# New keys for single tasks of a planned kernel, packed chunks of x, and a state update in column halves

## The chip, the cores and the metric

The kernel runs on one NeuronCore of a Trainium2 chip. Five engines work from queues of their own: TensorE (PE in the profile; PEld is its weight load), VectorE (DVE), ScalarE (ACT), GpSimd (POOL) and SyncE (SP), which here issues every DMA. The metric is the device time of one execution in microseconds (us), as a median of runs.

## The reference

The program is a gated linear recurrence over 768 steps for 4 batches of 8 heads (head size 48), and behind it a feed-forward layer without a token mixer:

```python
for t in range(S):
    state = alpha[:, :, t, :, None] * state + np.einsum('bhd,bhe->bhde', k[:, :, t], v[:, :, t])
    y[:, :, t] = np.einsum('bhd,bhde->bhe', q[:, :, t], state)
x = y.transpose(0, 2, 1, 3).reshape(B * S, H * D)      # 3072 x 384
h = x @ w_in                                           # 384 -> 2048
g = h * np.tanh(log1p(exp(h)))
out = g @ w_out                                        # 2048 -> 384
```

The weights arrive as 64-bit floats.

## The kernel before

**Chunks.** Time is cut into chunks of 128 steps, six for each of the four batches; the 24 chunks go by number n, batches innermost, so chunks 0 to 3 begin the four batches. For a chunk, q, k and alpha of all heads arrive as one tile `qka` (112 partitions, 1541 numbers each) and v as another. VectorE makes the running products of alpha with two scans: `rest` (L492) from the chunk's end and the front one (L509); it multiplies k (L504, two halves) and q (L519) by them. TensorE makes scores (L539, 16 small matmuls), VectorE masks them (L549, two instructions), TensorE makes the product y (L594; 16 matmuls in the first chunk of a batch, 24 later). For the next chunk the state is advanced: TensorE turns k (L702), ScalarE copies it out (L706), TensorE multiplies it with v (L711, four matmuls whose 112x96 results hold two heads each, of which only the two blocks on the diagonal are wanted), and two instructions (L721 on ScalarE in a batch's first chunk, L723 on VectorE later) gather the diagonal blocks into the state.

**x in two parts.** y is kept as an upper part (rounded, L611) and a lower part (what is left). In chunks 0 to 7 the lower part is made by TensorE (L623) and ScalarE (L631), later by VectorE (L616). The rows of the last head pair are then moved to other partitions by six DMAs a chunk (L637), 16 KB each. Only then can the chunk's matmuls with w_in begin.

**Weights.** For each of 16 tiles f of 128 hidden columns, a DMA (L349) brings both weight matrices' parts; VectorE makes 32-bit floats from the 64-bit words in three steps (L364, L369, L374), ScalarE rounds an upper part (L379), and the lower part comes from TensorE and ScalarE (L403, L404, L407) for f < 4, from VectorE (L393) for the others. The weights are loaded a second time later (L422), and ScalarE checks them (L431, L434).

**Units.** A unit is two or four chunks of x by one tile f: nine matmuls with w_in into a PSUM bank `h` (L754; there are two such banks), five ScalarE and three VectorE instructions for the activation (L762 to L788; L762 and L772 are the ones that read the bank), and three matmuls with w_out for each chunk (L816) that add into the banks `o0` to `o3`. There are 106 units: 20 of two chunks, then 86 of four.

**Order.** No loop sets the order. All of this is first recorded as tasks, each with an engine, a cost, a time after which its result is there, and a key. `Plan.order` then plays a clock: on each engine it looks at the first 150 waiting tasks by key and takes the one that can begin first (the earlier key where two can), writes down the order, and the kernel issues the instructions in it. The engines then run it strictly in that order. Where TensorE would be idle between `FILL_FROM` and `FILL_UNTIL` the planner puts a matmul on zeros in (a fill, L866), which computes nothing. `EARLY_BANKS` gives the PSUM banks of the first chunks by hand. A DMA is a task of SP with a fixed cost and a fixed delay.

Of the kernel before, what the change touches and what calls it, by code (L numbers as in the profile page):

```python
# [37 lines left out]
QKA = (3 * C + 1) * NPAIR + 1  # L38

# [26 lines left out]
EARLY_BANKS = {
    0: "o2 h o3 o0 att att".split(),
    1: "att att att att o3 att".split(),
    2: "o0 h h h att o1".split(),
    3: "o3 h att o1 att o0".split(),  # L70
    4: "att att att att o1 h".split(),
    5: "o2 o3 att o2 o2 att".split(),
}
# [7 lines left out]
BEGIN = {"PE": 2.4, "DVE": 4.3, "ACT": 2.2, "POOL": 4.2, "SP": 1.2}  # L81
# [17 lines left out]
class Plan:  # L99
# [23 lines left out]
    def order(self):  # L123
# [95 lines left out]
WINDOW = 150  # L219

COST = {
    "load part": (0.7, 3.3), "load q": (1.8, 5.0), "load v": (0.7, 4.0), "load w": (2.0, 5.0),
    "move": (0.63, 2.5), "store": (0.47, 3.0),
    "cold fill": (0.321, 0.36), "fill": (0.1635, 0.2), "off": (0.2, 0.35), "w off": (0.95, 1.2), "lead": (0.27, 0.38), "bits": (0.47, 0.58), "w hi": (0.42, 0.56), "w lo": (0.95, 1.08),
# [3 lines left out]
    "scores": (1.07, 1.08), "y0": (1.08, 1.1), "y": (1.7, 1.7), "turn": (0.4, 0.64),  # L228
    "turned": (0.43, 0.57), "update": (0.76, 0.98),
# [14 lines left out]
def fast_path(ctx, tc, qka, v, w, out, good):  # L244
# [57 lines left out]
    xs = [const.tile([P, 2, NPAIR, k * C], F32R, name=f"xs{i}") for i, k in enumerate(X_TILES)]  # L302
# [40 lines left out]
    def weight(f):  # L343
        key = weight_unit[f] - W_LEAD
# [9 lines left out]
        got = add("SP", *COST["load w"], max(key, FIRST_W + f) - 4, load, uses=[stage])  # L354
        fs = slice(f * P, (f + 1) * P)
        for m in range(2):
# [29 lines left out]
            k = key + 0.5 * m  # L386
# [29 lines left out]
    def weight_check(f):  # L416
        key = CHECK_FROM + f * CHECK_STEP
# [30 lines left out]
    def attention(n):  # L448
# [3 lines left out]
        st, key = state[b], due[n]  # L452
# [23 lines left out]
        if n == 0:  # L476
# [7 lines left out]
        got_v = add("SP", *COST["load v"], key - V_LEAD, load_v, uses=[v_buf])  # L484
# [255 lines left out]
    def unit(c0, nt, f, at, ends):  # L740
        N, key = nt * C, float(at)
# [398 lines left out]
```

## Time and profile before

| | |
|---|---|
| median of three runs | 524.3 us (522.8 to 524.36) |
| the profiled execution's own time | 526.62 us |
| its span, first to last instruction | 524.9 us |
| PE busy | 513.0 us, 98% of the span |
| DVE busy | 382.3 us, 73% |
| ACT busy | 397.3 us, 76% |
| matmuls on zeros (L866) | 43 |

Busy time of PE counts every matmul from its issue to its modelled end, the ones on zeros too, and matmuls overlap; so the share of 98% says that PE has nearly always something in it, not that it could not be faster. What counts is how far apart the starts are. Durations below come from the profiled execution.

### The profile page before, as it was taken

Reading aid. Unit: us, or ns where it says so; the run is one execution under the profiler, and the core shown is the slowest. Engines: PE = TensorE matmul, PEld = TensorE weight load, DVE = VectorE, ACT = ScalarE, POOL = GpSimd, SP = SyncE. Lnnn points to the kernel's source line nnn. Section 1 sums busy time; section 2 is a strip of 40 time slices with the busy share of each in tenths; the row PEclk is TensorE's granted clock in tenths of the full one; section 3 lists DMA queues with packets and bytes.
Section 4 is the critical chain, followed back from the end, with each engine's and each line's share of the span. In section 5 each row is a group of like instructions: output and inputs, shape, how many; then the busy total and the mean of one; then the engine's idle time right before and its main releaser. Section 6 shows DMA issues by size and latency. Waiting matters only on the chain.

```text
span 524.9 us, 11178 instructions
## 1 busy us (share of the span) xinstructions
PE 513.0 (98%) x4287; PEld 447.7 (85%) x4287; DVE 382.3 (73%) x743; ACT 397.3 (76%) x914; POOL 4.6 (1%) x34
## 2 busy tenths in 40 slices
PE   6999999999999999899999999999999999999996
PEld 4678989998898888788899888899988899999996
DVE  6899999999976876868777566886468654554452
ACT  1578789999699987888867856577776567787774
POOL 2000000000000000000000000000000000000000
PEclk9799999999999999999999999999999999999999
DMA  8656636413254866465320132220042000010001
GB/s 269 179 172 195 200 82 205 166 61 116 68 177 139 233 229 191 169 204 162 112 76 0 47 92 76 76 76 1 1 136 78 9 9 2 15 46 1 1 1 65
DMA packets 21818, 54.31 MB, mean 103 GB/s; under 512 B 4000, under 2 KB 14752, under 8 KB 21760
## 3 DMA queue, kind: packets, MB, share of 16 engines
q1 hardware_dynamic: 21760, 53.55, 33.2%
q8 instruction: 35, 0.57, 0.5%
q14 instruction: 23, 0.19, 0.1%
HBM read 46.45 MB, written 4.72 MB: 97 GB/s over the span
## 4 chain that ended last, share of the span: by engine, by line
PE 79%; DMA 8%; DVE 7%; SPq 3%; issue 2%; ACT 2%; DVEq 0%; ACTq 0%
PE bank L816 33%; PE bank L754 32%; DMA qka<-in_qka_dram 8%; PE bank L594 5%; PE bank L539 3%; SPq L637 2%; PE bank L711 2%; PE bank L702 1%; PE bank L403 1%; DVE rest L492 1%; DVE qka L509 1%; DVE t L781 1%; DVE y L772 1%; DVE g L788 1%; DVE xs L616 1%
## 5 line engine op out<-in xcount | busy, mean ns | idle before, releaser
L816 PE MATMUL bank<-wo,g 128*128 128x384 f32 x1152 | 227.4, 341 | 0.2 <-DVE part L843 0.2
L754 PE MATMUL bank<-xs,wi 128*128 128x512 f32 (+1 forms) x954 | 217.8, 373 | 1.8 <-DVE y L772 1.8
L816 PEld LDWEIGHTS bank<-wo,g 128*128 128x128 f32 x1152 | 198.3, 188 | 7.6 <-DVE part L843 0.4
L754 PEld LDWEIGHTS bank<-xs,wi 128*128 128x128 f32 x954 | 167.4, 188 | 28.9 <-DVE y L772 2.1
L762 ACT ACTIVATE u<-bank 128x512 f32<-128x512 f32 (+1 forms) x106 | 58.9, 555 | 82.7 <-PE bank L754 82.4
L772 DVE SCALAR_TENSOR_TENSOR y<-u,bank 128x512 f32<-128x512 f32 (+1 forms) x106 | 66.8, 631 | 49.2 <-ACT u L762 48.8
L788 DVE TENSOR_TENSOR g<-t,g 128x512 fp32r<-128x512 f32 (+1 forms) x106 | 67.2, 635 | 48.0 <-ACT g L785 47.8
L775 ACT ACTIVATE t<-t,tenth 128x512 f32<-128x512 f32 (+1 forms) x106 | 72.0, 679 | 2.3
L781 DVE SCALAR_TENSOR_TENSOR t<-y,t 128x512 f32<-128x512 f32 (+1 forms) x106 | 67.0, 633 | 5.1 <-ACT t L778 4.3
L768 ACT ACTIVATE t<-u 128x512 f32<-128x512 f32 (+1 forms) x106 | 62.6, 590 | 3.7 <-DVE g L788 1.4
L785 ACT ACTIVATE g<-t 128x512 fp32r<-128x512 f32 (+1 forms) x106 | 61.5, 581 | 5.1 <-DVE t L781 3.2
L778 ACT ACTIVATE t<-t 128x512 f32<-128x512 f32 (+1 forms) x106 | 61.6, 581 | 0.5
L492 DVE TENSOR_TENSOR_SCAN rest<-qka,behind 112x516 f32<-112x516 f32 x24 | 29.5, 1228 | 15.2 <-DMA qka<-in_qka_dram 15.2
L509 DVE TENSOR_TENSOR_SCAN qka<-qka,ahead 112x516 f32<-112x516 f32 x24 | 29.4, 1223 | 0.0
L549 DVE COPY_PREDICATED probs<-causal,bank 128x384 f32<-128x384 uint32 x48 | 25.8, 584 | 4.4 <-PE bank L539 4.1
L594 PEld LDWEIGHTS bank<-probs,v 128*64 128x64 f32 (+3 forms) x768 | 20.6, 128 | 8.5 <-issue 3.9
L594 PE MATMUL bank<-probs,v 128*64 128x64 f32 (+3 forms) x768 | 25.5, 227 | 1.5 <-DVE ahead L497 1.5
L539 PEld LDWEIGHTS bank<-qka 48*64 48x64 f32 x768 | 18.6, 137 | 5.8 <-issue 3.7
L539 PE MATMUL bank<-qka 48*64 48x64 f32 (+1 forms) x768 | 22.3, 255 | 0.0
L762 ACT ACTIVATION_READ_ACCUMULATOR u<-bank 128x1 f32 x106 | 20.7, 195 | 0.0
L611 ACT ACTIVATE xs<-bank 112x256 fp32r<-112x256 f32 x48 | 16.3, 373 | 5.6 <-PE bank L594 5.6
L711 PEld LDWEIGHTS bank<-v,ks 128*112 128x112 f32 x160 | 18.0, 177 | 1.8 <-ACT xs L631 0.5
(79 smaller groups left out, 348.4 us busy)
## 6 DMA issues: line engine op xcount, KB each, us to landing
qka<-in_qka_dram SPq DMA_DIRECT2D x23, 674.2 KB, 5.5
ws<-in_wp_dram SPq DMA_DIRECT2D x16, 768.0 KB, 4.6
wc<-in_wp_dram SPq DMA_DIRECT2D x16, 768.0 KB, 5.1
v<-in_vp_dram SPq DMA_DIRECT2D x24, 192.0 KB, 4.6
out_dram<-osb SPq DMA_DIRECT2D x16, 192.0 KB, 1.8
xs<-xs SPq DMA_DIRECT2D x144, 16.0 KB, 2.5
out_dram<-part SPq DMA_DIRECT2D x8, 192.0 KB, 3.1
qka<-in_qka_dram SPq DMA_DIRECT2D x2, 224.0 KB, 3.7
```

The source lines that it names most:

```text
L539: nc.tensor.matmul(p[a][to, i, blocks], K()[r : r + D, j, to], q.rearrange("p (x t) -> p x t", t=HALF), start=True, stop=True,)
L594: made = nc.tensor.matmul(o, l, r, start=begins, stop=m >= len(ops) - 2, skip_group_check=True)
L754: nc.tensor.matmul(p[:, :N], wi[:, z, s, fs], x[:, a, s], start=m == 0, stop=m == len(passes) - 1)
L762: nc.scalar.activation(wide(u), wide(h), AF.Exp, scale=-1.0, accum_out=uchk[:, at : at + 1])
L768: nc.scalar.activation(wide(t), wide(u), AF.Square, bias=1.0, scale=2.0)
L772: nc.vector.scalar_tensor_tensor(wide(y), wide(u), 0.5, wide(h), ALU.add, ALU.mult)
L775: nc.scalar.activation(wide(t), wide(t), AF.Ln, bias=tenth, scale=0.1)
L778: nc.scalar.activation(wide(t), wide(t), AF.Exp, scale=-1.0)
L781: nc.vector.scalar_tensor_tensor(wide(t), wide(y), 0.4, wide(t), ALU.mult, ALU.mult)
L785: nc.scalar.activation(g.tile[:, 0, :N], wide(t), AF.Copy)
L788: late[mybir.EngineType.DVE] = nc.vector.tensor_tensor(g.tile[:, 1, :N], wide(t), g.tile[:, 0, :N].bitcast(F32), ALU.subtract)
L816: made = nc.tensor.matmul(o.tile[:, :DM], g.tile[:, a, j * C : (j + 1) * C], wo[:, z, f], start=begins and m == 0, stop=end and m == 2,)
```

## The change

- **Keys.** A table `SHIFT` adds a number to the keys of single chunks, units, weight tiles and second weight loads. `EARLY_BANKS` has other banks and two more chunks.
- **DMAs in the planner.** A load's delay is no longer fixed: the planner adds up the transfers in their order and lets no more than eight be under way. Costs are changed to match.
- **Loads.** Chunk 1's `qka` is loaded in two parts, alpha first. The rows of `qka` in DRAM lie 1664 numbers apart and no longer 1541.
- **x.** A chunk's upper and lower part now lie next to each other in `xs`, so a move (L637 before, L667 now) takes one run of 256 numbers a partition instead of two of 128. The matmuls with w_in read x in pieces of 128 columns that are 256 apart.
- **State update.** Each pair's matmul with a 112x96 result is cut into two with results of 64x48 and 48x48, each from half the columns of k. The wanted blocks then stand in the same columns, and one gather of 112x192 takes the place of two of 48x192.
- **Weights.** The lower parts come from TensorE for f < 3 instead of f < 4; for f = 3 VectorE makes them.

The order of instructions as built, with chunk numbers as in the words; `qka_116` is chunk 0's tile, `qka_128` (before) and `qka_120` (after) are chunk 1's, `v_124` is chunk 0's v, `v_139` and `v_130` chunk 1's, `ws` are weight loads. SP from its first DMA on, before:

```order
L470 DMA qka_116<-in_qka_dram 112x517
L470 DMA qka_116<-in_qka_dram 112x512 x2
L474 DMA v_124<-in_vp_dram 128x384
L465 DMA qka_128<-in_qka_dram 112x1541
L474 DMA v_139<-in_vp_dram 128x384
L349 DMA ws_145<-in_wp_dram 128x1536
L349 DMA ws_179<-in_wp_dram 128x1536
L465 DMA qka_218<-in_qka_dram 112x1541
```

The same place after:

```order
L498 DMA qka_116<-in_qka_dram 112x517
L498 DMA qka_116<-in_qka_dram 112x512 x2
L498 DMA qka_120<-in_qka_dram 112x517
L502 DMA v_124<-in_vp_dram 128x384
L498 DMA qka_120<-in_qka_dram 112x1024
L502 DMA v_130<-in_vp_dram 128x384
L377 DMA ws_135<-in_wp_dram 128x1536
L377 DMA ws_139<-in_wp_dram 128x1536
L493 DMA qka_217<-in_qka_dram 112x1541
```

Chunk 1's alpha moved ahead of chunk 0's v; the rest keeps its order.

PE around its first unit, before: `qka_313` is chunk 3's tile, `w_lead_1_363` weight tile 1's and `w_lead_0_439` weight tile 2's.

```order
L403 MATMUL bank<-w_lead_1_363,ident 128x384
L404 MATMUL bank<-wo,minus_ident 128x384
L539 MATMUL bank<-qka_313 64x128 x2
L539 MATMUL bank<-qka_313 64x64 x2
L539 MATMUL bank<-qka_313 64x2x64 x2
L539 MATMUL bank<-qka_313 64x64 x2
L539 MATMUL bank<-qka_313 64x128 x2
L539 MATMUL bank<-qka_313 64x64 x2
L539 MATMUL bank<-qka_313 64x2x64 x2
L539 MATMUL bank<-qka_313 64x64 x2
L754 MATMUL bank<-xs_111,wi 128x256 x9
L403 MATMUL bank<-w_lead_0_439,ident 128x384
```

The same place after, from the end of chunk 2's state update on: `v_226` and `ks_351` are chunk 2's, `w_lead_1_371` weight tile 1's, `qka_323` chunk 3's.

```order
L743 MATMUL bank<-v_226,ks_351 64x48
L743 MATMUL bank<-v_226,ks_351 48x48
L782 MATMUL bank<-xs_111,wi 128x256 x9
L653 MATMUL bank<-xs_111,minus_ident 112x256 x2
L431 MATMUL bank<-w_lead_1_371,ident 128x384
L432 MATMUL bank<-wo,minus_ident 128x384
L570 MATMUL bank<-qka_323 64x128 x2
L570 MATMUL bank<-qka_323 64x64 x2
L570 MATMUL bank<-qka_323 64x2x64 x2
L570 MATMUL bank<-qka_323 64x64 x2
```

The first unit moved from behind chunk 3's scores to ahead of chunk 2's lower part, of weight tile 1 and of those scores. Over the whole program 36 matmuls on zeros stand in PE's order after, 43 before.

SP where chunk 13's `qka` is loaded, before (`qka_2772`; `wc` are second weight loads):

```order
L422 DMA wc_2665<-in_wp_dram 128x1536
L422 DMA wc_2702<-in_wp_dram 128x1536
L637 DMA xs_111<-xs_111 16x2x128 x6
L465 DMA qka_2772<-in_qka_dram 112x1541
L474 DMA v_2806<-in_vp_dram 128x384
```

The same place after (`qka_2735`):

```order
L450 DMA wc_2634<-in_wp_dram 128x1536
L450 DMA wc_2688<-in_wp_dram 128x1536
L667 DMA xs_111<-xs_111 16x256 x6
L493 DMA qka_2735<-in_qka_dram 112x1541
L450 DMA wc_2749<-in_wp_dram 128x1536
```

Six moves still stand ahead of the load; a second weight load moved in behind it, ahead of v. The diff, cut to its core:

```diff
+QKA_ROW = 1664
...
-COLD = 16
+COLD = 14
...
-    0: "o2 h o3 o0 att att".split(),
+    0: "att o0 o2 att o3 att".split(),
...
+SHIFT = {
+    "chunk": {
+        4: -3, 5: -1, 6: 1, 7: 3, 8: -0.1, 12: 0.01, 20: 2.5, 21: 1,
...
-W_PE = 4
-W_DVE = 4
+W_PE = 3
+W_DVE = 3
...
+                    if e == "SP" and len(landed) >= QUEUE:
+                        r = max(r, landed[-QUEUE])
...
+            if e == "SP":
+                moving = max(moving, at + DMA_FIRST) + t.late
+                landed.append(moving + DMA_LAST)
+                t.late = moving + DMA_LAST - at
...
-    xs = [const.tile([P, 2, NPAIR, k * C], F32R, name=f"xs{i}") for i, k in enumerate(X_TILES)]
+    xs = [const.tile([P, NPAIR, k, 2, C], F32R, name=f"xs{i}") for i, k in enumerate(X_TILES)]
...
-        st, key = state[b], due[n]
+        st, key = state[b], due[n] + SHIFT["chunk"].get(n, 0.0)
...
-            nc.sync.dma_start(t, qka[b, c])
+            nc.sync.dma_start(t, qka[b, c, :, :QKA])
...
+        elif n == 1:
+            got_a = add("SP", *COST["load part"], -98.7, load_part(2 * NPAIR * C, QKA), uses=[q_buf])
+            got_k = got_q = add("SP", *COST["load qk"], -98.5, load_part(0, 2 * NPAIR * C), uses=[q_buf])
...
-                    x[48 + r : 64 + r, :, s, tok].bitcast(F32),
-                    x[r + 16 * s : r + 16 * s + 16, :, NK, tok].bitcast(F32),
+                    x[48 + r : 64 + r, s, place].bitcast(F32),
+                    x[r + 16 * s : r + 16 * s + 16, NK, place].bitcast(F32),
...
-                nc.tensor.matmul(
-                    p[:R, j, : 2 * D], ks_buf.tile[:, j], V()[:, 2 * D * j : 2 * D * (j + 1)],
-                    start=True, stop=True,
-                )
...
+                for a, wide in ((0, HALF), (1, D)):
+                    h = (2 * j + a) * D
+                    nc.tensor.matmul(
+                        p[64 * a : 64 * a + wide, j, :D], ks_buf.tile[:, j, 64 * a : 64 * a + wide],
+                        V()[:, h : h + D], start=True, stop=True,
+                    )
+
+        def gather():
+            u = by_pair(u_buf.tile)[:R, :, :D]
+            if first:
+                nc.scalar.copy(by_head, u)
+            else:
+                nc.vector.tensor_tensor(by_head, u, by_head, ALU.add)
...
-                    p[:, :N], wi[:, z, s, fs], x[:, a, s], start=m == 0, stop=m == len(passes) - 1
+                    p[:, :N], wi[:, z, s, fs], x[:, s, :, a], start=m == 0,
+                    stop=m == len(passes) - 1,
...
-    qka = np.zeros((B, NCH, R, QKA), inputs["q"].dtype)
+    qka = np.zeros((B, NCH, R, QKA_ROW), inputs["q"].dtype)
```

## Rows read from the trace of the kernel before

**Rows 1.** The page, busy time of the engines
```profile
PE 513.0 (98%) x4287; PEld 447.7 (85%) x4287; DVE 382.3 (73%) x743; ACT 397.3 (76%) x914; POOL 4.6 (1%) x34
```

**Rows 2.** Windows: length, busy time by engine, granted clock, DMA share, GB/s
```profile
12.10:20.60 8.50, 8.40 (x82) 5.35 (x82) 7.03 (x15) 3.75 (x10) 0.00 (x0) 0.60 0.53 146
...
31.30:180.00 148.70, 148.70 (x1348) 133.81 (x1347) 139.67 (x302) 131.56 (x337) 0.53 (x6) 1.00 0.49 154
```

**Rows 3.** Timeline of PE to 48 us: start, length, engine, line, count, [idle]
```profile
12.15 1.06 PE L594 MATMUL bank<-probs,v 128*64 128x64 f32 x32 [1.53 <-DVE ahead L497]
...
15.61 1.56 PE L539 MATMUL bank<-qka 48*64 48x128 f32 x32
...
32.67 1.34 PE L754 MATMUL bank<-xs,wi 128*128 128x256 f32 x9
...
43.55 0.81 PE L403 MATMUL bank<-w_lead,ident 128*128 128x384 f32 x2
...
44.46 0.66 PE L594 MATMUL bank<-qka,state 48*48 48x128 f32 x16
...
46.04 0.91 PE L403 MATMUL bank<-w_lead,ident 128*128 128x384 f32 x2
...
46.97 0.40 PE L623 MATMUL bank<-xs,minus_ident 112*112 112x256 f32 x2
```

**Rows 4.** Timeline of DVE to 40 us, three of its waits from chunk 1 on
```profile
9.93 1.23 DVE L492 TENSOR_TENSOR_SCAN rest<-qka,behind 112x516 f32<-112x516 f32 x1 [2.23 <-DMA qka<-in_qka_dram]
...
17.24 1.05 DVE L549 COPY_PREDICATED probs<-causal,bank 128x384 f32<-128x384 uint32 x2 [0.76 <-PE bank L539]
...
25.95 1.06 DVE L549 COPY_PREDICATED probs<-causal,bank 128x384 f32<-128x384 uint32 x2 [0.87 <-PE bank L539]
```

**Rows 5.** DMA issues from 0.8 to 0.9, and from 2.6 to 3.0 us: size, us to landing
```profile
qka<-in_qka_dram SPq DMA_DIRECT2D x1, 226.2 KB, 2.9
...
qka<-in_qka_dram SPq DMA_DIRECT2D x1, 674.2 KB, 7.2
```

**Rows 6.** Who waited for whom, PE: total us, times, longest
```profile
PE bank L754 <- DVE y L772: 1.8, 1, 1.8
...
PE bank L702 <- DVE xs L616: 0.9, 3, 0.4
```

**Rows 7.** Timelines of SP, DVE and PE around 200 to 213 us
```profile
199.73 5.07 SPq L637 DMA_DIRECT2D xs<-xs  x6
204.91 0.52 SPq L465 DMA_DIRECT2D qka<-in_qka_dram  x1
...
210.61 1.23 DVE L492 TENSOR_TENSOR_SCAN rest<-qka,behind 112x516 f32<-112x516 f32 x1 [3.65 <-DMA qka<-in_qka_dram]
...
202.76 2.25 PE L816 MATMUL bank<-wo,g 128*128 128x384 f32 x12
204.94 0.90 PE L539 MATMUL bank<-qka 48*64 48x128 f32 x32
205.77 4.40 PE L754 MATMUL bank<-xs,wi 128*128 128x512 f32 x18
```

**Rows 8.** Timeline of PE, a state update (L711) and its neighbours at 220 us
```profile
220.62 2.25 PE L816 MATMUL bank<-wo,g 128*128 128x384 f32 x12
222.70 2.24 PE L754 MATMUL bank<-xs,wi 128*128 128x512 f32 x9
...
226.75 0.93 PE L711 MATMUL bank<-v,ks 128*112 128x96 f32 x8
227.46 0.77 PE L816 MATMUL bank<-wo,g 128*128 128x384 f32 x3
```

**Rows 9.** The gathers by line and form: count, busy us, mean ns, idle
```profile
L723 DVE TENSOR_TENSOR state<-bank,state 48x192 f32<-48x192 f32 x32 | 11.3, 352 | 5.9 <-PE bank L711 5.7
```

**Rows 10.** Timelines: DVE's last lower part of w_in, PE's first use of it
```profile
149.39 0.56 DVE L393 TENSOR_TENSOR wi<-w_lead,wi 128x384 fp32r<-128x384 f32 x1
...
153.63 1.55 PE L754 MATMUL bank<-xs,wi 128*128 128x512 f32 x6
```

More of the change, by code (lines that the diff above doesn't have):

```diff
@@ L61 @@
 CHECK_STEP = 2.0
-COLD = 16
+COLD = 14
 FILL_BANKS = ("o3", "o2", "o1", "o0", "h", "att")
-FILL_FROM, FILL_UNTIL = 2.4, 130.0
+FILL_FROM, FILL_UNTIL = 2.5, 130.0
 FILL_MARGIN = 0.1
 EARLY_BANKS = {
-    0: "o2 h o3 o0 att att".split(),
[L68 to L72, printed above, removed]
+    0: "att o0 o2 att o3 att".split(),
+    1: "att att o3 o0 att att".split(),
+    2: "o2 att o0 att h att".split(),
+    3: "att o3 att h h o1".split(),
+    4: "att o3 att att att att".split(),
+    5: "att att att o3 att att".split(),
+    6: "att att att att h o1".split(),
+    7: "att att att att o0 o2".split(),
+}
+SHIFT = {
+    "chunk": {
+        4: -3, 5: -1, 6: 1, 7: 3, 8: -0.1, 12: 0.01, 20: 2.5, 21: 1,
+    },
+    "unit": {
[3 rows of a table added]
+    },
+    "weight": {
+        0: -3, 1: -1, 2: 1.5, 3: 1.1, 4: 5.7, 7: 2, 9: 5, 10: -2, 11: 2, 12: 0.3, 13: 0.5, 15: 2,
+    },
+    "weight check": {
+        5: 9.5, 6: 10, 7: -12, 8: -2, 9: 6, 10: -5,
+    },
 }
 X_PE = 8
-W_PE = 4
-W_DVE = 4
+W_PE = 3
+W_DVE = 3
 W_PE_BANKS = ["o2"]
@@ L132, in order @@
         done, n, port_free = [], len(self.tasks), 0.0
+        moving, landed = 0.0, []
         def ready(t):
@@ L219 @@
 WINDOW = 150
+QUEUE = 8
+DMA_FIRST, DMA_LAST = 1.4, 0.8
 COST = {
-    "load part": (0.7, 3.3), "load q": (1.8, 5.0), "load v": (0.7, 4.0), "load w": (2.0, 5.0),
-    "move": (0.63, 2.5), "store": (0.47, 3.0),
-    "cold fill": (0.321, 0.36), "fill": (0.1635, 0.2), "off": (0.2, 0.35), "w off": (0.95, 1.2), "lead": (0.27, 0.38), "bits": (0.47, 0.58), "w hi": (0.42, 0.56), "w lo": (0.95, 1.08),
+    "load part": (0.47, 0.62), "load qk": (0.47, 1.2), "load q": (0.47, 1.75),
+    "load v": (0.47, 0.54), "load w": (0.45, 1.9), "move": (0.47, 0.055), "store": (0.47, 0.54),
+    "cold fill": (0.321, 0.36), "fill": (0.1635, 0.2), "off": (0.125, 0.3), "w off": (0.95, 1.2), "lead": (0.27, 0.38), "bits": (0.47, 0.58), "w hi": (0.42, 0.56), "w lo": (0.95, 1.08),
     "w check": (0.92, 1.2),
@@ L227 @@
     "state": (0.365, 0.4), "state0": (0.31, 0.35), "mask": (0.49, 0.63),
-    "scores": (1.07, 1.08), "y0": (1.08, 1.1), "y": (1.7, 1.7), "turn": (0.4, 0.64),
-    "turned": (0.43, 0.57), "update": (0.76, 0.98),
+    "scores": (1.02, 1.05), "y0": (1.1, 1.2), "y": (1.77, 1.79), "turn": (0.42, 0.64),
+    "turned": (0.43, 0.57), "update": (0.7, 0.9),
     "x hi": (0.275, 0.415), "x lo": (0.34, 0.455),
@@ L343, in weight @@
     def weight(f):
-        key = weight_unit[f] - W_LEAD
+        key, shift = weight_unit[f] - W_LEAD, SHIFT["weight"].get(f, 0.0)
         stage = plan.buffer("stage")
@@ L352, in load @@
             )
-        got = add("SP", *COST["load w"], max(key, FIRST_W + f) - 4, load, uses=[stage])
+        got = add("SP", *COST["load w"], max(key, FIRST_W + f) - 4 + shift, load, uses=[stage])
         fs = slice(f * P, (f + 1) * P)
@@ L416, in weight_check @@
     def weight_check(f):
-        key = CHECK_FROM + f * CHECK_STEP
+        key = CHECK_FROM + f * CHECK_STEP + SHIFT["weight check"].get(f, 0.0)
         again = plan.buffer("stage")
@@ L481, in attention @@
             )
+        elif n == 1:
+            got_a = add("SP", *COST["load part"], -98.7, load_part(2 * NPAIR * C, QKA), uses=[q_buf])
+            got_k = got_q = add("SP", *COST["load qk"], -98.5, load_part(0, 2 * NPAIR * C), uses=[q_buf])
         else:
             got_a = got_k = got_q = add("SP", *COST["load q"], key - Q_LEAD, load, uses=[q_buf])
-        got_v = add("SP", *COST["load v"], key - V_LEAD, load_v, uses=[v_buf])
+        got_v = add("SP", *COST["load v"], -98.6 if n == 0 else key - V_LEAD, load_v, uses=[v_buf])
         def scan_rest():
@@ L740, in unit @@
     def unit(c0, nt, f, at, ends):
-        N, key = nt * C, float(at)
+        N, key = nt * C, at + SHIFT["unit"].get(at, 0.0)
         tile_at, place = X_AT[c0]
-        x = xs[tile_at][:, :, :, place * C : place * C + N]
+        x = xs[tile_at][:, :, place : place + nt]
         fs = slice(f * P, (f + 1) * P)
```

19 lines of the change are left out of this document (4 added, 15 removed), and 3 rows, old and new, of the table SHIFT.

## The prediction

> **What bounds the kernel now.** I read the page's busy times first: PE 98% of the span, the others about 75% [rows 1]. Since busy time counts matmuls on zeros and waits that are shorter than the pipeline, I went on to the windows, and there the program has two parts. From 31.3 to 180 us PE has something in every microsecond, at full clock, and none of it is zeros; VectorE is at 139.67 of 148.7 us beside it [rows 2]. From there to the end PE is still the engine that sets the time: its listed waits are few, 1.8 and 0.9 us for the longest two lines [rows 6]. So from 31 us on a microsecond of PE's work that goes is a microsecond of the time, as long as VectorE keeps up. Before 31 us it is the other way round. The timeline of PE shows waits and zeros between its pieces there, for example 1.53 us ahead of the first product [rows 3], and VectorE's timeline shows why: it waits 2.23 us for chunk 1's `qka`, and later 0.76 and 0.87 us for scores [rows 4]. After the 1.53 us of idle PE the granted clock is lower: 0.60 in the mean from 12.1 to 20.6 us [rows 2], and chunk 1's scores take 1.56 us where 0.90 us is their length at full clock [rows 3, 7]. That is what lengthens the 0.76 us wait.
>
> **The change, part by part.** I sum against the profiled execution's own 526.62 us (span 524.9, and 1.7 around it), which lies 2.3 us above the median 524.3 of the runs; the difference I find is then taken off the median.
>
> *One weight tile less on TensorE.* For f = 3 two groups go, each of one matmul at L403 and one at L404. They stand where PE is full: from 43.55 to 44.46 and from 46.04 to 46.97 us [rows 3], so 0.91 + 0.93 = 1.84 us. The two ScalarE copies behind them go too and give nothing, ScalarE is not the bound. VectorE gets two more lower parts of 0.56 us [rows 10], 1.1 us, and loses 16 of 32 gathers of 0.35 us [rows 9], five of them in chunks 4 to 8, before the weights are done: 1.75 us. VectorE's other work hides nothing here, it simply comes out 0.6 us shorter; were its load the bound, the two lower parts alone would cost 1.1 us.
>
> *The state update in halves, 20 times.* Before, eight passes take 0.71 us from start to start (226.75 to 227.46), and they do not hold up what follows [rows 8]. After, there are 16 passes of half the width. The nearest row is a product in a batch's first chunk: 32 passes in 1.06 us, half of them with the same 128 rows by 64 columns of weights and 64 moving columns, against 48 now [rows 3]. So 0.53 us for 16 as an equal share, and by width three quarters of that, 0.40 us. But a stretch of such column-split matmuls has to be entered: twelve matmuls of L816 take 2.18 us when scores follow (202.76 to 204.94) and 2.08 us when a unit follows (220.62 to 222.70) [rows 7, 8], so the entry costs 0.10 us. Bounds: 0.10 + 0.40 = 0.50 us a time, which is 0.21 less than before, and, if the passes take the same 0.71 us in sum and leaving costs as much as entering, 0.91 us, which is 0.20 more. The nearest row is the product, with 0.53 + 0.10 and something for leaving: I take 0.65 us, 0.06 less, which makes 1.2 us in 20; ends -4.2 and +4.0.
>
> The Trainium skill, TensorEngine Tiling, section Key Properties, says that changing the tiling mode, not just the tile, drains the array; this speaks against cutting a matmul in halves when its neighbours are whole. The 0.10 us at the entry agrees. By the rule alone, without credit for narrower passes, each update would come out dearer and the 20 would add up to 4 us; by the row of the product they save 1.2.
>
> *The front, up to 31 us.* VectorE's order up to chunk 3's products is the same, so its timeline before can be used. It was free at 7.70 us and waited until 9.93 for 674 KB of chunk 1 [rows 4], issued behind 866 KB (sizes by the shapes in the order) and landing 7.2 us after its issue [rows 5]. Now only the alpha part, 226 KB, has to be there, with 674 KB ahead of it. The first 226 KB landed 2.9 us after their issue at 0.8 us, at 3.7; 1540 KB were in by 9.9 us; so 900 KB are in at about 3.7 + 6.2 x 674/1314 = 6.9 us, before 7.7. The wait of 2.23 us goes. With it goes PE's idle stretch ahead of the first product, and if the clock does not fall, the 0.76 us as well. What is late next: chunk 2's `qka`, which can be issued no earlier than before, since it waits for chunk 0's buffer and for the weights ahead of it, and then chunk 3's, behind six moves. I give back 0.5 us for these: VectorE is 2.5 us earlier at chunk 3. Ends: 0, if the next loads take all of it, and 3.9, if all three waits go. Beside this, PE's first unit (1.34 us, at 32.67 [rows 3]) now stands ahead of chunk 3's scores, where PE would wait for VectorE or do zeros, and no longer behind them: 1.2 us. The 43 matmuls on zeros become 36, which is the same gain seen from the other side and is not counted again. Front: 2.5 + 1.2 = 3.7 us; ends 0 and 5.1.
>
> *Moves, loads and keys behind 180 us.* The clearest stall is at 210 us. SyncE spends 5.07 us on six moves, then issues chunk 13's `qka` at 204.91; VectorE stands 3.65 us until it lands, and the `h` bank that the next unit needs is not emptied: PE waits 1.8 us [rows 6, 7]. After, the six moves still stand ahead of that load, but each is one run a partition. A load with one run a partition took SyncE 0.52 us there, a move 5.07/6 = 0.85 us. If the moves go to 0.52, the load is issued 2 us earlier. Other small waits for PSUM banks (0.9 us) depend on where the keys put the units. Of 1.8 + 0.9 = 2.7 us I take half, 1.4; ends 0 and 2.7. That x is now read in pieces 256 columns apart I cost at nothing: L623 reads x in two pieces as it is and its two matmuls take 0.40 us, against 1.34 us for nine unbroken ones of the same width [rows 3], so a further one is (1.34 - 0.40)/7 = 0.13 us, with no dearer first two.
>
> Sum: 1.84 + 1.2 + 3.7 + 1.4 = 8.1 us. Own time 526.6 - 8.1 = 518.5; median 524.3 - 8.1 = 516.2 us.
>
> **Rivals.** *The loads hold the front.* SyncE is one queue, and chunks 2 and 3 and two weight tiles come through it however early VectorE is. For it: VectorE's first wait is for a DMA, and 7.2 us to landing against 2.9 for the first part shows the queueing [rows 4, 5]. Against it: the other two waits are for scores, not for loads. Also VectorE then reaches the last weight tile late: its lower part is made at 149.39 to 149.95 and used at 153.63 us [rows 10], 3.7 us of room, while PE comes there some 5 us earlier. Then the front gives 1.0 instead of 3.7 and the stalls at 200 us stay: 524.3 - 1.84 - 1.2 - 1.0 = 520.3 us.
>
> *The halves cost more than the whole.* At the upper end of the update's price it adds 4.0 instead of taking 1.2: 516.2 + 5.2 = 521.4 us. For it: the 0.10 us at the entry [rows 7]. Against it: the product's 1.06 us for 32 passes [rows 3].
>
> *Units in a row wait for their banks: slower.* There are two `h` banks, and a third unit's matmuls with w_in can start only when ScalarE and VectorE have read the first. PE's order before has two units' L754 behind each other with nothing between (18 matmuls) in two places, by the order as built; the second is the one at 205.77 us, and the unit next after it is the one that waited 1.8 us [rows 6, 7]. After, there are eight such places, six of them with four-chunk units and one of these with three units in a row. If each of the six costs 1.8 us and the gain of 1.4 is gone, the time is 516.2 + 1.4 + 10.8 = 528.4 us. It decides from four of six on: (8.1 - 1.4)/1.8 = 3.7. Against it: the wait at 210 us came when VectorE was held by a load; two units in a row alone are emptied while the downward matmuls run.
>
> **How the numbers follow.** Forecast 0.56 (511 to 519), loads 0.20 (520.3), halves 0.08 (521.4), units in a row 0.08 (528.4), and 0.08 for small gains and stalls that cancel within 0.3%. That bound, 1.6 us, is about what a measurement of this kernel can tell from no change. Faster than 522.7 are the first three, except some of the halves: 0.82. Same: 0.10. Slower: 0.08. The best ends of all four terms together would be 1.84 + 4.2 + 5.1 + 2.7 = 13.8 us, the worst a loss of 2.2; the range takes 511 to 523.5, which leaves out the slower rival and the joint best end.
>
> **What would show it.** In the profile after: VectorE's scan of chunk 1 starts at about 7.7 us with no DMA wait; the granted clock stays at full from 12 to 20 us; the first unit on PE starts near 27 us instead of 32.67, and chunk 4's product near 40 instead of 44.46; the update takes 0.6 to 0.7 us from start to start; moves are issued 0.5 us apart; no wait of 1.8 us on `h` at 205 us. I would be wrong if VectorE's wait for chunk 1 is only handed on to chunk 2 or 3, if updates take over 0.8 us, or if PE's waits for `h` add up to more than 5 us.

## The result, and the profile after

The changed kernel takes 530.2 us (528.3 to 531.2, four runs) against 523.75 us beside it: ratio 1.012, interval 1.0085 to 1.0155. It is slower by some 6 us, and the forecast was 516.2 us. The profiled execution took 531.16 us, with a span of 529.5 us.

The page's busy times after (engine, us, share of the span, instructions) answer to [rows 1]:

```profile
PE 510.0 (96%) x4434; PEld 439.1 (83%) x4434; DVE 377.0 (71%) x729; ACT 393.6 (74%) x908; POOL 4.6 (1%) x34
```

PE has 3 us less to do and stands still more: 19.5 us of the span are not covered, against 11.9 before. The windows (stretch, its length, busy time of each engine, granted clock, DMA share, GB/s) say where, and answer to [rows 2]:

```profile
12.10:20.60 8.50, 7.30 (x104) 4.61 (x102) 6.36 (x14) 3.88 (x11) 0.00 (x0) 1.00 0.73 205
31.30:180.00 148.70, 145.90 (x1347) 128.56 (x1346) 137.34 (x296) 124.65 (x322) 0.53 (x6) 0.99 0.44 142
52.70:64.90 12.20, 10.35 (x120) 8.88 (x119) 9.22 (x20) 6.91 (x19) 0.00 (x0) 0.86 0.60 166
```

The clock in the front is full now (1.00 for 0.60). But the long stretch, in which PE had no gap before, has 2.8 us of gaps, 1.85 of them in twelve microseconds at 53 to 65 us, with the clock at 0.86 there. PE's timeline (start, duration, instruction, idle time before it and what ended it) has both parts, and answers to [rows 3, 8]:

```profile
26.52 1.34 PE L782 MATMUL bank<-xs,wi 128*128 128x256 f32 x9
...
40.85 0.66 PE L625 MATMUL bank<-qka,state 48*48 48x128 f32 x16
...
55.17 0.67 PE L743 MATMUL bank<-v,ks 128*64 128x48 f32 x16
55.77 0.80 PE L845 MATMUL bank<-wo,g 128*128 128x384 f32 x3
...
57.47 0.51 PE L845 MATMUL bank<-wo,g 128*128 128x384 f32 x2
59.53 0.97 PE L845 MATMUL bank<-wo,g 128*128 128x384 f32 x4 [1.55 <-DVE g L817]
60.80 1.55 PE L570 MATMUL bank<-qka 48*64 48x128 f32 x32 [0.30 <-DVE qka L550]
62.28 1.01 PE L732 MATMUL bank<-ident,qka 112*128 112x112 f32 x4
62.97 1.31 PE L845 MATMUL bank<-wo,g 128*128 128x384 f32 x3
...
251.36 0.60 PE L732 MATMUL bank<-ident,qka 112*128 112x112 f32 x4 [0.87 <-DVE xs L646]
251.73 1.29 PE L845 MATMUL bank<-wo,g 128*128 128x384 f32 x6
254.10 0.67 PE L743 MATMUL bank<-v,ks 128*64 128x48 f32 x16 [1.07 <-ACT ks L736]
```

The front came as forecast: the first unit at 26.52 us, chunk 4's product at 40.85, an update in 55.77 - 55.17 = 0.60 us. Then PE waits 1.55 us, up to 59.53 us, for a gate `g` of VectorE. Behind the wait the scores take 1.55 us where 0.90 is their length at full clock. VectorE's timeline has the reason, and answers to [rows 4]:

```profile
7.63 1.22 DVE L523 TENSOR_TENSOR_SCAN rest<-qka,behind 112x516 f32<-112x516 f32 x1
...
17.74 1.23 DVE L523 TENSOR_TENSOR_SCAN rest<-qka,behind 112x516 f32<-112x516 f32 x1 [2.14 <-DMA qka<-in_qka_dram]
...
52.52 0.42 DVE L817 TENSOR_TENSOR g<-t,g 128x256 fp32r<-128x256 f32 x1
55.67 1.23 DVE L523 TENSOR_TENSOR_SCAN rest<-qka,behind 112x516 f32<-112x516 f32 x1 [2.72 <-DMA qka<-in_qka_dram]
...
193.95 1.23 DVE L523 TENSOR_TENSOR_SCAN rest<-qka,behind 112x516 f32<-112x516 f32 x1 [1.50 <-DMA qka<-in_qka_dram]
```

Chunk 1's scan no longer waits, chunk 2's does (2.14 us), and chunk 6's scan stands 2.72 us with the gates of two units queued behind it. SyncE's DMA issues after (start, time spent issuing) show why that load was late, and answer to [rows 7]:

```profile
45.43 3.69 SPq L667 DMA_DIRECT2D xs<-xs  x6
49.23 0.51 SPq L493 DMA_DIRECT2D qka<-in_qka_dram  x1
...
195.85 3.67 SPq L667 DMA_DIRECT2D xs<-xs  x6
```

Six moves go out ahead of chunk 6's `qka`. In the kernel before that load was issued at 45.25 us, ahead of the same moves, and its scan did not wait, by SyncE's and VectorE's timelines of before:

```profile
45.25 0.33 SPq L465 DMA_DIRECT2D qka<-in_qka_dram  x1
...
48.23 4.22 SPq L637 DMA_DIRECT2D xs<-xs  x6
```

```profile
56.04 1.22 DVE L492 TENSOR_TENSOR_SCAN rest<-qka,behind 112x516 f32<-112x516 f32 x1
```

Before, the load took 5.6 us to land, at 50.85, and so had 5.2 us to spare. After, it is issued 4.0 us later and takes 6.4 us, 0.8 more. The front's gain uses up the rest: VectorE now wants the chunk at 55.67 - 2.72 = 52.95 us, 3.1 us earlier than before. Together that is 4.0 + 0.8 + 3.1 - 5.2 = 2.7 us, the wait.

A second kind of stall sits on ScalarE, whose timeline has a check of the weights' second load at 247 us:

```profile
247.04 0.90 ACT L459 ACTIVATE wc<-wc 128x768 f32<-128x768 f32 x1 [2.87 <-DMA wc<-in_wp_dram]
```

What ScalarE does for the units and for L736 queues behind it, and PE's waits of 0.87 and 1.07 us at 251 to 254 us follow from it. In the list of waits after (line, releaser: us in total, times, longest) the DMA rows are:

```profile
DVE rest L523 <- DMA qka<-in_qka_dram: 21.3, 14, 3.4
...
ACT wc L459 <- DMA wc<-in_wp_dram: 7.4, 3, 4.0
```

Before, the second was 0.2 us, and the first:

```profile
DVE rest L492 <- DMA qka<-in_qka_dram: 15.2, 12, 3.6
```

Setting PE's starts against those before at equal work (matmuls weighted by their length), after is 5.0 us ahead at 32 us of the kernel before, 3.6 ahead at 53, 0.3 behind at 65, 2.2 behind from 259 us and 4.2 behind from 366 us to the end. (That is less than 6 us because the profiled execution of before, 526.62 us, was 2.9 us above the median beside it, and that of after 1.0 above its own.)

### The profile page after: what moved, and what is told of

Same layout as the page of the kernel before. It is cut to its first block, busy times and chain, and to the rows that moved or that the text cites. A ratio compares the mean times of both kernels' runs of the same rounds, so it can differ in the third digit from the quotient of the medians.

```text
span 529.5 us, 11398 instructions
## 1 busy us (share of the span) xinstructions
PE 510.0 (96%) x4434; PEld 439.1 (83%) x4434; DVE 377.0 (71%) x729; ACT 393.6 (74%) x908; POOL 4.6 (1%) x34
## 4 chain that ended last, share of the span: by engine, by line
PE 63%; DMA 14%; DVE 9%; ACT 6%; SPq 3%; issue 2%; POOL 0%; DVEq 0%; ACTq 0%; POOLq 0%
PE bank L845 28%; PE bank L782 27%; DMA qka<-in_qka_dram 10%; PE bank L625 4%; SPq L667 3%; DMA wc<-in_wp_dram 3%; PE bank L570 2%; DVE rest L523 2%; DMA xs<-xs 2%; DVE qka L540 1%; ACT t L804 1%; DVE t L810 1%; DVE g L817 1%; ACT wc L459 1%; PE bank L732 1%
## 5 line engine op out<-in xcount | busy, mean ns | idle before, releaser
L845 PE MATMUL bank<-wo,g 128*128 128x384 f32 x1152 | 226.3, 342 | 2.3 <-DVE g L817 1.9
L845 PEld LDWEIGHTS bank<-wo,g 128*128 128x128 f32 x1152 | 199.2, 189 | 10.4 <-DVE g L817 2.9
L523 DVE TENSOR_TENSOR_SCAN rest<-qka,behind 112x516 f32<-112x516 f32 x24 | 29.6, 1232 | 21.5 <-DMA qka<-in_qka_dram 21.3
L570 PE MATMUL bank<-qka 48*64 48x128 f32 (+1 forms) x768 | 22.3, 255 | 0.6 <-DVE qka L550 0.5
L459 ACT ACTIVATE wc<-wc 128x768 f32<-128x768 f32 x16 | 14.6, 912 | 7.4 <-DMA wc<-in_wp_dram 7.4
```

The lines of the kernel that those rows point to most:

```text
L570: nc.tensor.matmul(p[a][to, i, blocks], K()[r : r + D, j, to], q.rearrange("p (x t) -> p x t", t=HALF), start=True, stop=True,)
L845: made = nc.tensor.matmul(o.tile[:, :DM], g.tile[:, a, j * C : (j + 1) * C], wo[:, z, f], start=begins and m == 0, stop=end and m == 2,)
```

## The experiments

Three theories. **P**: the planner's new DMA costs are below the measured ones, so loads are put behind moves or begun too late, and the in-order engines stand. **K**: the shifted keys are themselves a worse order. **M**: one of the edits to the instructions is dear. The trace after gives P its numbers: issues of moves are 3.67/6 = 0.61 us apart (the planner has 0.47), and a load of `qka` lands in 5.3 us in the median and 4.6 at the least (the planner has 1.4 + 1.75 + 0.8 = 3.95 for one alone).

All runs, each ratio to the kernel before measured beside it; the last column is VectorE's wait for `qka` (for the scan `rest`) in the profiled execution, us:

| kernel | median us | ratio, interval | waits |
|---|---|---|---|
| before | 524 | | 15.2 |
| after | 530.2 | 1.012, 1.0085 to 1.0155 | 21.3 |
| e1 after, DMA costs and model of before | 522.65 | 0.9977, 0.995 to 1.0004 | 8.4 |
| e2 edits alone (planner, costs, keys, banks of before) | 520.9 | 0.9942, 0.9917 to 0.9967 | 9.6 |
| e3 after without shifted keys | 538.9 | 1.0297, 1.0244 to 1.035 | 28.4 |
| e4 after, measured DMA costs | 520.6 | 0.9925, 0.9896 to 0.9955 | 7.9 |
| e5 after, measured moves alone | 528.9 | 1.0077, 1.0051 to 1.0104 | 22.1 |
| e6 after, measured loads alone | 528.7 | 1.0084, 1.0056 to 1.0111 | 21.6 |
| e7 edits with the whole update | 521.7 | 0.9962, 0.9939 to 0.9986 | 8.6 |
| e9 edits without the split load | 524.2 | 1.0, 0.9982 to 1.0018 | 9.1 |
| e10 after, loads pulled forward | 522.9 | 0.9982, 0.9957 to 1.0006 | 4.7 |
| e12 e4, loads pulled forward | 520.5 | 0.9931, 0.9905 to 0.9958 | 3.7 |
| e13 before, loads pulled forward | 521.7 | 0.9971, 0.9948 to 0.9995 | 8.2 |
| e8 after, DMA costs above the measured | 518.8 | 0.9911, 0.9882 to 0.9941 | 3.5 |
| e15 e8, loads pulled forward | 521.4 | 0.9949, 0.9928 to 0.997 | 0 |
| e14 e2, loads pulled forward | 525.3 | 1.0008, 0.998 to 1.0035 | 7.3 |
| e16 edits, four weight tiles on TensorE | 523.4 | 0.9992, 0.9965 to 1.0018 | 8.6 |
| e17 edits, x and moves of before | 520.95 | 0.995, 0.9925 to 0.9976 | 9.0 |

**Which part is slow: costs, keys or edits.** e1 is after with the DMA costs of before and without the transfer model:

```diff
-                    if e == "SP" and len(landed) >= QUEUE:
-                        r = max(r, landed[-QUEUE])
...
-            if e == "SP":
-                moving = max(moving, at + DMA_FIRST) + t.late
-                landed.append(moving + DMA_LAST)
-                t.late = moving + DMA_LAST - at
...
-    "load part": (0.47, 0.62), "load qk": (0.47, 1.2), "load q": (0.47, 1.75),
-    "load v": (0.47, 0.54), "load w": (0.45, 1.9), "move": (0.47, 0.055), "store": (0.47, 0.54),
+    "load part": (0.7, 3.3), "load qk": (1.2, 4.2), "load q": (1.8, 5.0), "load v": (0.7, 4.0), "load w": (2.0, 5.0),
+    "move": (0.63, 2.5), "store": (0.47, 3.0),
```

> The changed kernel with the planner's DMA costs of before (a load of qka is there 5.0 us after it begins, a weight load 5.0, a move takes 0.63 us of SyncE and 2.5 to land; no limit of eight), all else as changed: keys, banks, packed x, halves, weights. Theory P, the new DMA costs are too low for the chip (a move 0.47 us planned and about 0.62 measured, a load of qka 4 us planned and 5.3 measured), so loads are put behind moves and the engines that run in order wait: 515 to 520 us, front gain kept, no wait of 2.7 us on VectorE at 53 us. Theory K, the keys themselves put the work in an order that stalls, whatever the DMA costs: 526 us or more. Theory M, one of the edits that do not touch the order loses the time: 529 to 531 us.

e2 goes on from e1: the keys, banks, other costs and start times of before too, so that only the edits to loads, x, update and weights are left. e3 is after without the keys alone.

```diff
+SHIFT = {"chunk": {}, "unit": {}, "weight": {}, "weight check": {}}
...
-BEGIN = {"PE": 2.55, "DVE": 3.3, "ACT": 2.4, "POOL": 4.2, "SP": 0.8}
+BEGIN = {"PE": 2.4, "DVE": 4.3, "ACT": 2.2, "POOL": 4.2, "SP": 1.2}
```

> The planner, its costs, keys, banks and starting times of before; of the change only packed x, the state update in halves with one gather, weight tile 3 to VectorE, the split load of chunk 1 and the padded rows. Theories P and K: 524 less 1.8 for the weight tile, 2.4 for the updates (0.60 us each in the profile after, 0.715 before) and up to 2.5 for the front: 517 to 521 us. Theory M: 526 us or more.

> The changed kernel with an empty table of shifts, its new DMA costs and banks kept. Theory P: the loads still come late, 524 to 532 us. Theory K: 516 to 521 us, and the waits at 57 and 250 us go. Theory M: 529 to 531 us.

e4 is after with measured DMA costs:

```diff
-DMA_FIRST, DMA_LAST = 1.4, 0.8
+DMA_FIRST, DMA_LAST = 1.5, 0.9
...
-    "load part": (0.47, 0.62), "load qk": (0.47, 1.2), "load q": (0.47, 1.75),
-    "load v": (0.47, 0.54), "load w": (0.45, 1.9), "move": (0.47, 0.055), "store": (0.47, 0.54),
+    "load part": (0.47, 0.62), "load qk": (0.47, 1.2), "load q": (0.47, 2.45),
+    "load v": (0.47, 0.78), "load w": (0.45, 2.55), "move": (0.62, 0.17), "store": (0.47, 0.54),
```

> The changed kernel with its new way to count DMAs, but with the transfer times that the profile after shows one behind the other: qka 2.45 us (1.75 planned), weights 2.55 (1.9), v 0.78 (0.54), a move 0.62 us of SyncE and 0.17 of transfer (0.47 and 0.055), 2.4 us from issue to the end besides (2.2). Theory P: 515 to 520 us. Theory K: 526 us or more. Theory M: 529 to 531 us.

A few numbers of the planner, and no edit to an instruction, take the kernel from 530.2 to 520.6 us. K falls: without the keys it is 538.9 us. M falls: the edits alone make the kernel before faster, 520.9 us. The sizes were missed: e1 and e4 come out above the 515 to 520 us that P gave, e3 above every range given. And the keys are not shown to win anything by themselves: with the DMA costs of before, e1 has keys, banks and the other costs and is no faster than e2 without them (522.65 against 520.9 us).

**Which of the costs.** e5 has e4's cost of a move alone, e6 the rest of e4's numbers without it:

```diff
-    "load v": (0.47, 0.54), "load w": (0.45, 1.9), "move": (0.47, 0.055), "store": (0.47, 0.54),
+    "load v": (0.47, 0.54), "load w": (0.45, 1.9), "move": (0.62, 0.17), "store": (0.47, 0.54),
```

> The changed kernel with one planner cost altered: a move at 0.62 us of issue and 0.17 us of transfer (measured: issue 0.51 to 0.64 us apart) instead of 0.47 and 0.055; the load costs stay too low. Theory P-moves (the loads stand behind six moves because the planner thinks a batch of moves short): most of the 9.6 us between the changed kernel and the one with all measured costs comes back, 521 to 524 us, VectorE's waits for qka under 12 us. Theory P-loads (the planner believes that a load lands 0.7 to 1 us sooner than it does and so issues it too late): under half comes back, 526 to 530 us, VectorE's waits for qka still over 16 us.

> The changed kernel with the planner's load costs as measured (qka 2.45, weights 2.55, v 0.78 us of transfer, 1.5 and 0.9 us ahead and behind) and the moves as changed (0.47, 0.055). Theory P-loads: 520 to 523 us, VectorE's waits for qka under 12 us, ScalarE's for the weights' second load under 3 us. Theory P-moves: 526 to 530 us, qka waits over 16 us. If both this and the run with the moves alone come out near 521, either cost suffices to move the load of chunk 6 ahead of the six moves.

Neither is enough; I had expected one of them to carry it. In both the six moves still stand ahead of chunk 6's load. But so they do in e4, and in the fastest kernel below, e8 (the load is issued at 51.00, 50.20, 49.10 and 48.37 us in e5, e6, e4 and e8); this one place does not tell a slow order from a fast one. VectorE's timeline of e5, of e6 and of e4 reads at that scan:

```profile
57.49 1.23 DVE L523 TENSOR_TENSOR_SCAN rest<-qka,behind 112x516 f32<-112x516 f32 x1 [1.96 <-DMA qka<-in_qka_dram]
```

```profile
56.62 1.23 DVE L523 TENSOR_TENSOR_SCAN rest<-qka,behind 112x516 f32<-112x516 f32 x1 [2.25 <-DMA qka<-in_qka_dram]
```

```profile
55.19 1.23 DVE L523 TENSOR_TENSOR_SCAN rest<-qka,behind 112x516 f32<-112x516 f32 x1 [1.11 <-DMA qka<-in_qka_dram]
```

In e8 the scan waits 1.24 us there. The planner's answer to costs is not a sum of answers. So costs don't separate "loads late" from "another order altogether", and the next runs leave the order of all other engines alone.

**The loads alone, at a fixed order.** e10 is the changed kernel with one step after the planning; e12, e13, e14 and e15 do the same to e4, before, e2 and e8.

```diff
     tasks = plan.order()
+    for tag in ("qka",):
+        q = plan.queues[tag]
+        for i in range(plan.slots[tag], len(q)):
+            of = lambda u: [j for j, z in enumerate(tasks) if u in z.uses]
+            at, now = max(of(q[i - plan.slots[tag]])[-1], of(q[i - 1])[0]) + 1, of(q[i])[0]
+            tasks.insert(at, tasks.pop(now))
```

> The changed kernel, its planner, costs, keys and banks untouched; after the planning each qka load from chunk 2 on is pulled forward on SyncE to right behind the last use of the buffer that it takes. Only SyncE's order changes (chunk 6's load stands behind one move instead of six), all other engines keep theirs. Theory P (the order on the other engines is good, in-order VectorE just waits for loads that stand behind moves): VectorE's waits for qka fall from 21.3 to under 12 us, no 2.72 us wait at 53 us, and the time is 520 to 525 us. Theory O (the order that the planner writes for the other engines with its keys and costs is itself the worse one; the waits for loads are covered or only change places): 527 to 531 us.

7.3 us come back by SyncE's order alone. SyncE's issues in e10 at the place shown above for after, and then VectorE's and PE's timelines there:

```profile
45.49 0.51 SPq L667 DMA_DIRECT2D xs<-xs  x1
46.37 0.33 SPq L493 DMA_DIRECT2D qka<-in_qka_dram  x1
46.76 3.03 SPq L667 DMA_DIRECT2D xs<-xs  x5
```

```profile
52.57 0.42 DVE L817 TENSOR_TENSOR g<-t,g 128x256 fp32r<-128x256 f32 x1
52.91 1.23 DVE L523 TENSOR_TENSOR_SCAN rest<-qka,behind 112x516 f32<-112x516 f32 x1
```

```profile
57.52 1.21 PE L845 MATMUL bank<-wo,g 128*128 128x384 f32 x6
58.65 0.90 PE L570 MATMUL bank<-qka 48*64 48x128 f32 x32
59.48 0.60 PE L732 MATMUL bank<-ident,qka 112*128 112x112 f32 x4
59.85 1.29 PE L845 MATMUL bank<-wo,g 128*128 128x384 f32 x6
```

Up to 57.5 us both run alike, in the same order. From there to the L845 behind the transposes (L732) PE takes 2.33 us here and 62.97 - 57.47 = 5.50 us in after. So VectorE's one wait of 2.72 us costs PE 3.17 us: 1.85 us of idle time, and 1.3 us at the lower clock.

The Trainium skill, DMA: Bandwidth & Descriptors, Rules for kernel authors, says to issue a DMA early and wait on its semaphore late. In e10 this case agrees, by 7.3 us; in e12 below it gives nothing, and in e15 it costs 2.6 us.

> The kernel before, with its qka loads from chunk 2 on pulled forward on SyncE to right behind the last use of the buffer that they take; all else as before. Theory P: VectorE's waits for qka fall from 15.2 to 8 to 10 us (the 2.2 us for chunk 1 stays), the 3.65 us wait at 207 us goes, and the time comes down by 1 to 4 us, 520.5 to 523.5 us. Theory O: within 1 us of before.

The kernel before had some of it too: 1.5 us (0.9971), waits 8.2 us.

> The changed kernel planned with the measured DMA costs (520.6 us), and in addition each qka load from chunk 2 on pulled forward on SyncE to right behind the last use of its buffer. Theory P: its waits of VectorE for qka are already down to 7.9 us, half of them in the first 60 us where the load waits for the buffer and not for moves, so 0 to 3 us are left to gain: 518 to 520.6 us. Theory O: no change within 1 us, or slower where six moves now wait behind a load that waits for its buffer (521 to 523 us).

No change within the runs: 520.5 against 520.6 us, although VectorE's waits for `qka` fall from 7.9 to 3.7 us. So a wait of VectorE is not by itself time lost. e8 is e4 with more room:

```diff
-    "load part": (0.47, 0.62), "load qk": (0.47, 1.2), "load q": (0.47, 2.45),
-    "load v": (0.47, 0.78), "load w": (0.45, 2.55), "move": (0.62, 0.17), "store": (0.47, 0.54),
+    "load part": (0.47, 0.62), "load qk": (0.47, 1.2), "load q": (0.47, 3.0),
+    "load v": (0.47, 1.0), "load w": (0.45, 2.9), "move": (0.62, 0.17), "store": (0.47, 0.54),
```

> The changed kernel planned with DMA costs above the measured ones (qka 3.0, weights 2.9, v 1.0 us of transfer; moves as measured). Theory P: loads are planned with room, VectorE's waits for qka stay at 5 to 10 us, 517 to 521 us. Theory O (the planner's order reacts to any change of cost by several us either way): anything from 518 to 528 us, with qka waits that don't follow the costs.

e8, planned with room for every load, has the lowest median, 518.8 us, and beats both kernels; its interval overlaps those of e4 and e2. Its list of VectorE's waits has one DMA row:

```profile
DVE rest L523 <- DMA qka<-in_qka_dram: 3.5, 4, 1.5
```

> The changed kernel planned with DMA costs above the measured ones (518.8 us), and each qka load from chunk 2 on pulled forward on SyncE to right behind the last use of its buffer. By theory P its VectorE waits for qka are only 3.5 us already, so at most 1 to 2 us are left: 517 to 519 us.

> The kernel with the change's mechanical edits and the planner, costs and keys of before (520.9 us), and each qka load from chunk 2 on pulled forward on SyncE to right behind the last use of its buffer. Against the kernel before with the same pull (521.7 us) it tells what the mechanical edits are worth when no load stands behind moves. If the prediction's terms hold (1.8 + 1.2 + 3.7): 515 to 517 us. If the kernel before's stalls and the edits' gain overlap, or the front's gain is lost again by 60 us: 518.5 to 521 us.

Both of these went the wrong way, and against P in its simple form: fewer waits for `qka`, more time. Both also miss the ranges given for them. The pulled load waits on SyncE for its buffer, and now the moves and other loads wait behind it. PE's timeline of e15:

```profile
81.51 1.51 PE L782 MATMUL bank<-xs,wi 128*128 128x256 f32 x9 [1.26 <-DMA xs<-xs]
...
201.80 2.53 PE L782 MATMUL bank<-xs,wi 128*128 128x512 f32 x10 [1.12 <-DMA xs<-xs]
```

and SyncE's issues ahead of the second wait, where three moves come behind the load:

```profile
192.97 1.78 SPq L667 DMA_DIRECT2D xs<-xs  x3
196.09 0.33 SPq L493 DMA_DIRECT2D qka<-in_qka_dram  x1
196.46 1.77 SPq L667 DMA_DIRECT2D xs<-xs  x3
```

In e14 v and a weight tile, issued behind a pulled load, come late, by SyncE's timeline, PE's and VectorE's:

```profile
36.16 0.33 SPq L470 DMA_DIRECT2D qka<-in_qka_dram  x1
36.59 0.37 SPq L354 DMA_DIRECT2D ws<-in_wp_dram  x1
37.01 0.44 SPq L479 DMA_DIRECT2D v<-in_vp_dram  x1
```

```profile
44.12 0.64 PE L720 MATMUL bank<-v,ks 128*64 128x48 f32 x16 [2.21 <-DMA v<-in_vp_dram]
```

```profile
43.21 0.36 DVE L369 TENSOR_SCALAR w_lead<-ws 128x384 int32<-128x384 int32 x1 [2.23 <-DMA ws<-in_wp_dram]
```

In e2 this v went out at 31.77 us, ahead of the load. These waits explain a part of e14 only: at equal work PE is 3.8 us behind e2 by 28 us, before them, and 6.1 us behind after them. There chunk 2's load landed 1.3 us later than in e2 behind the same DMAs, and the granted clock was 0.74 from 24 to 34 us, 1.00 in e2. The runs of e14 reach from 520.4 to 528.9 us, so what the pull alone costs there is not shown.

So loads first is not right everywhere: where the load at the head of the one queue must wait for its buffer, it holds DMAs that are wanted sooner.

**The prediction's terms, one by one.** Each undoes one edit in e2; the padded rows of `qka` were not undone by themselves. e7 the halves (and the one gather, by the two of before):

```diff
-                for a, wide in ((0, HALF), (1, D)):
-                    h = (2 * j + a) * D
-                    nc.tensor.matmul(
-                        p[64 * a : 64 * a + wide, j, :D], ks_buf.tile[:, j, 64 * a : 64 * a + wide],
-                        V()[:, h : h + D], start=True, stop=True,
-                    )
+                nc.tensor.matmul(
+                    p[:R, j, : 2 * D], ks_buf.tile[:, j], V()[:, 2 * D * j : 2 * D * (j + 1)],
+                    start=True, stop=True,
+                )
...
```

> The kernel with the change's mechanical edits and the planner, costs and keys of before, in which the state update is whole again (8 passes of 128 columns and two gathers, as before the change). By the starts in the trace of after (update 0.59 to 0.60 us against 0.715 us) the halves save 0.12 us in each of 20: 2.4 us, so 520.9 + 2.4 = 523.3 us. By the prediction's price (0.06 each): 522.1. If the halves cost more than the whole (the rival): under 520.5 us.

e9 the split load of chunk 1 (and the key of chunk 0's v), e16 the weight tile f = 3, e17 the layout of x (and what writes, moves and reads it):

```diff
-        elif n == 1:
-            got_a = add("SP", *COST["load part"], -98.7, load_part(2 * NPAIR * C, QKA), uses=[q_buf])
-            got_k = got_q = add("SP", *COST["load qk"], -98.5, load_part(0, 2 * NPAIR * C), uses=[q_buf])
...
```

> The kernel with the change's mechanical edits and the planner, costs and keys of before, in which chunk 1's qka comes in one load again and chunk 0's v by its old key. If what the split gains in the front is kept to the end, as the prediction has it: 520.9 + 2.5 = 523.4 us, VectorE's wait of about 2.2 us ahead of chunk 1's scan back. If the front's gain is eaten by the loads of chunks 2 to 4 behind it (the rival that the loads hold the front): 520.4 to 521.8 us, with the lead over the kernel before the same from about 60 us on.

```diff
-W_PE = 3
-W_DVE = 3
+W_PE = 4
+W_DVE = 4
```

> The kernel with the change's mechanical edits and the planner, costs and keys of before (520.9 us), in which four weight tiles' low parts are made by TensorE again, as before the change. If the two groups of 0.91 and 0.93 us at full PE are worth their length, as the prediction has it: 520.9 + 1.8 = 522.7 us. If PE's waits take them up, or VectorE's two lower parts cost as much: 520 to 521.5 us.

```diff
-    xs = [const.tile([P, NPAIR, k, 2, C], F32R, name=f"xs{i}") for i, k in enumerate(X_TILES)]
+    xs = [const.tile([P, 2, NPAIR, k * C], F32R, name=f"xs{i}") for i, k in enumerate(X_TILES)]
...
```

> The kernel with the change's mechanical edits and the planner, costs and keys of before (520.9 us), with the layout of x and the six moves as before the change (two runs of 128 columns a partition instead of one of 256). If the layout is worth nothing on PE and the shorter issue of the moves (about 0.6 against 0.85 us) brings the load at 205 us forward, as the prediction has it: 521.5 to 523 us. If the moves' issue hardly differs: 520.5 to 521.5 us. If reading x in pieces costs PE something: under 520.3 us.

By the ratios against e2's 0.9942: halves 1.0 us, split load 3.0, weight tile 2.6, layout 0.4. Each, as a difference of two ratios, has 1.6 to 1.9 us on either side, so the halves and the layout alone are not told from nothing. They add up to 7.0 us, and all undone together (the kernel before) cost 3.0. The planner makes a new order for each, and that this accounts for the difference is not shown.

## Why the prediction was wrong

- **The step that failed** is the front's "What is late next", which gave back 0.5 us for chunks 2 and 3 and took the loads behind them at nothing. The sum treated 31 to 180 us as a stretch where "a microsecond of PE's work that goes is a microsecond of the time, as long as VectorE keeps up". That condition was named and not priced. SyncE's order of the changed kernel already had the six moves ahead of chunk 6's load, where before they stood behind it. Six moves are 3.7 us of delay, for a load that had 5.2 us to spare before and 2.1 once VectorE came 3.1 us earlier: the front's gain itself helped to make it late. That place cost 3.17 us; other late loads followed, at 194 and 247 us among them, and the `qka` loads pulled forward (e10, all else in its order) gave 7.3 us back. With them the kernel is level with before (0.9982) and not 8 us below; where the rest of the sum stays is open.
- **"Moves, loads and keys behind 180 us", 1.4 us of gain**: a loss of some 4 us instead. The one stall that it priced did go (PE's wait of 1.8 us for VectorE's `y` is 0.3 us after), but others came, of 1.15, 0.87, 1.07, 0.62 and 0.79 us between 195 and 353 us. The 5.07 us that I read for six moves [rows 7] was the longest row of six; ten of the 24 chunks' moves take 3.76 to 3.83 us before and ten 3.67 to 3.69 after (195.85 us in SyncE's rows above). So a longer run saves 0.02 us a move and not 0.85 - 0.52 = 0.33, and e17 measures nothing clear of noise. In SyncE's timeline of before:

```profile
251.96 3.78 SPq L637 DMA_DIRECT2D xs<-xs  x6
```

- **Weight tile, 1.84 us**: 2.6 in e16, with 1.9 on either side, so right as far as it can be told.
- **State update, 1.2 us**: 1.0 in e7. Its starts are 0.59 to 0.60 us apart against 0.71, some 0.12 us a time where I took 0.06, so 2.4 us are there on PE in 20; whether they are kept e7, with 1.8 us on either side, cannot tell. The Trainium skill, TensorEngine Tiling, Key Properties (a change of tiling mode drains the array) would have made it dearer. The trace shows it shorter, entering and leaving included, and with that the rival "the halves cost more than the whole" falls.
- **The front, 3.7 us**: won (5.0 us ahead at 32 us, the marks at 7.63, 26.52 and 40.85 us met) and kept in e2, where the split is worth 3.0 us. In after it was spent by 65 us. The prediction's own sign of being wrong, a wait only handed on to chunk 2, came true in VectorE's rows (2.14 us) and yet did not take the front's gain from PE.
- **Rivals.** "The loads hold the front" had the right queue and the wrong place: it looked at chunks 2 and 3 and could not end slower. "Units in a row", the one slower case, did not occur: PE's wait for `h` banks is 0.3 us in sum.

## What to carry to other kernels

Where one queue issues moves and loads in a fixed order, compare that order before and after first, and price each load that falls behind others by the issue time of what is ahead of it. An engine that comes earlier also wants its loads earlier: take a gain ahead of a load off that load's time to spare. Give a planner loads that are rather too long than too short: 0.2 to 0.7 us a load and 0.15 a move decided 9.6 us here, and only both together. Read an issue cost from the commonest group of a kind, not from the one at the clearest stall.

## What the runs showed of the hardware

- A move of 16 KB costs SyncE 0.61 us in runs of 256 columns and 0.63 us in two runs of 128 (six in 3.67 and 3.78 us): half the runs took 0.02 us off a move.
- After PE's 1.55 us of idle time at 58 us the granted clock fell from full to 0.65 in the mean of the next 4.5 us, between its levels of 2.4 and 1.2 GHz (windows as above):

```profile
59.50:64.00 4.50, 4.17 (x43) 3.71 (x44) 4.25 (x11) 3.33 (x9) 0.00 (x0) 0.65 0.21 61
55.67:59.50 3.83, 2.31 (x19) 1.94 (x15) 3.83 (x8) 0.73 (x3) 0.00 (x0) 1.00 0.87 211
```

- Sixteen passes of half the columns take 0.60 us (55.17 to 55.77 us after), eight whole ones 0.71 us (226.75 to 227.46 before [rows 8]), although whole-array matmuls (L845) stand on both sides of the sixteen.
